# One queue for the first weights of a gated feed-forward block, and a wait ahead of ScalarE's slices of x

## The chip, the cores and the metric

The kernel runs on one core of a Trainium2 chip. A core has a matrix engine (TensorE, PE in the profile, with its weight loads shown apart as PEld), a vector engine (VectorE, DVE), a scalar engine (ScalarE, ACT), a general engine (GpSimd, POOL) and an engine for synchronisation (SyncE, SP). Each engine works through its own program in order. SyncE, ScalarE and GpSimd also issue DMAs, each on a queue of its own; in the profile q1 is SyncE's queue, q10 ScalarE's and q0 GpSimd's. All queues are served by the same 16 DMA engines.

The metric is the device time of one execution, in microseconds (us). Before the change the median of three runs is 300.24 us (299.82 to 303.81).

## The reference

```python
B, S, D, F = 32, 32, 1024, 3584
# x: (B, S, D), w_gate and w_up: (D, F), w_down: (F, D), all bfloat16
def reference(x, w_gate, w_up, w_down):
    return (_gelu(x @ w_gate) * (x @ w_up)) @ w_down
```

With 1024 rows of x, this is two products 1024 x 1024 x 3584, a GELU (tanh form), an elementwise product, and one product 1024 x 3584 x 1024.

## The kernel before, in words

**Tiling.** The contraction over D is cut into 8 k-slices of 128. F is cut into 28 column chunks (m) of 128; chunks 0 to 7 (the "leading eight") have their weights in two large buffers, `wgbig` for gate and `wubig` for up, each loaded in eight DMAs of 256 KB, one per k-slice (`load_w0`, L285). The other twenty chunks come later, in groups of four, 1 MB per load. Rows of x are cut into pieces: XA (rows 0 to 255), XB1 and XB2 (128 rows each), XC2 (rows 512 to 1023).

**Getting x transposed.** TensorE needs x with the contraction index on the partitions. XA is loaded as two blocks of 128 rows (`xa`, one by SyncE, one by ScalarE, L290), turned on TensorE by products with an identity matrix (L351), and copied out of PSUM by VectorE (four copies) and ScalarE (one copy) at L300. The later pieces are loaded in four strips (L281), two strips per "side": SyncE brings side 0, ScalarE side 1, two DMAs per piece, so six for each of the two. VectorE then turns them with transposes at L460, one instruction per k-slice and piece, each waiting for both sides of its piece.

**The order of TensorE's work** is written out by hand in `steps`. After some warm-up products: the turning of XA; then chunks 0 to 7 on XA, all chunks together for k-slice 0, then for 1, and so on to 5, gate before up within a slice; then slices 6 and 7 chunk by chunk (parts 0 to 7). Then parts 8 to 11 (chunks 0 to 3 on rows 256 to 511): k-slices 0 to 3 first for XB1 alone (matmuls of 128 columns), then for XB2, and so on; after that everything part by part with 512 columns. Part 8 and those after it need the PSUM banks of parts 0 to 7 back, which VectorE frees. The second product, with `w_down`, follows (L417).

**ScalarE and VectorE behind it.** For every part ScalarE computes the GELU of the gate product into one of four buffers (L436), and VectorE multiplies it with the up product into `hT` (L469). VectorE's order is a list too (`mix`): E0 E1 E2 E3 (multiplications of parts 0 to 3), then A0 to A3 (XB1's transposes for k-slices 0 to 3), B0 to B3 (XB2's), E4, D4, D5 (both at once), and so on, later mixed with C0 to C7 (XC2's).

**The early loads.** `early_loads` is a generator that SyncE runs with side 0 and ScalarE with side 1. Each of the two loads its block of XA, then eight weight slices (SyncE gate, ScalarE up), then its strips of XB1, XB2 and XC2. A generator step ends at each `yield`; ScalarE counts the steps and after the ninth (`ACT_EARLY`), that is after its weights and ahead of its strips, does its PSUM copy. Nothing makes an x load wait. After its early loads ScalarE goes on to the GELUs, SyncE to the later weight groups, of which the first waits until all of x has landed.

Of the kernel before, what the change touches and what calls it, by code (L numbers as in the profile page):

```python
# [8 lines left out]
ACTF = mybir.ActivationFunctionType  # L9
# [75 lines left out]
def bass_standalone__geglu_ffn__sampling_kernel(  # L85
# [13 lines left out]
    DK = D // P  # L99
# [29 lines left out]
    XPIECES = [XB1, XB2, XC2]  # L129
    XA_PS = [(3, 0, 1), (4, 1, 2), (5, 2, 4), (6, 4, 6), (7, 6, 8)]  # L130
    XA_ACT = (4,)
    ACT_EARLY = 9


    parts = []
# [67 lines left out]
    def evac_eng_is_act(ji):  # L203
        return ji % 2 == 0
# [14 lines left out]
    Q_W0 = {(w, k): _Clock(f"{w}0k{k}", 16) for k in range(DK) for w in ("wg", "wu")}  # L219
# [8 lines left out]
    ctx = _Ctx()  # L228

    with ExitStack() as es:  # L230
# [8 lines left out]
        xa = hT[:, FM - 10:FM - 8, :]  # L239
# [38 lines left out]
        def load_x(ew, eng, q, side):  # L278
            c0, c1 = q[0] // 32, q[1] // 32
            for a in (2 * side, 2 * side + 1):  # L280
                v = ew.do(lambda: eng.dma_start(  # L281
                    xs[32 * a:32 * (a + 1), c0:c1, :], x_r[a, :, c0:c1, :]), clock=Q_X[(q, side)])
            ctx.set(("x", q, side), v)

        def load_w0(ew, eng, w, k):  # L285
            ctx.set((w + "0", k), ew.do(lambda: eng.dma_start(  # L286
                big[w][:, k, :], w_r[w][:, k, 0:NBIG * P]), clock=Q_W0[(w, k)]))

        def early_loads(ew, eng, side):
            yield ctx.set(("xa", side), ew.do(lambda: eng.dma_start(  # L290
                xa[:, side, :], xa_r[:, side, :]), clock=Q_XA[side]))
            for k in range(DK):
                yield load_w0(ew, eng, ("wg", "wu")[side], k)
            for q in XPIECES:
                yield load_x(ew, eng, q, side)

        def xa_copy(ew, j, copy):
            bank, k0, k1 = XA_PS[j]
            ew.wait(C_PE, ctx.get(("XP", j)))
            ctx.set(("XA", j), ew.do(lambda: copy(  # L300
                xT[:, k0:k1, XA[0]:XA[1]],
                ps[:, bank, 0:256 * (k1 - k0)].rearrange("p (k t) -> p k t", t=256))))
# [23 lines left out]
        def prog_sp(eng):  # L326
            sp = _Eng(ctx, eng, None)
            for _ in early_loads(sp, eng, 0):
                pass
            wd_mine = [k for k in range(len(wd_groups)) if k % 2 == 0]  # L330
            for j in range(NG):
                known_chunk = gate_w(sp, j)
                load_w(sp, eng, "wg", j)
                issue_wd(sp, eng, wd_mine, known_chunk, Q_WD_SP)
            issue_wd(sp, eng, wd_mine, FM, Q_WD_SP, force=True)
            ctx.set("wd_sp_total", Q_WD_SP.n)
            last = None
            for ji, (tc, col0, ncols, b) in enumerate(jobs):
                sp.wait(C_ACT if evac_eng_is_act(ji) else C_DVE, ctx.get(("E", ji)))
                last = sp.do(lambda: eng.dma_start(  # L340
                    out_r[:, tc, col0:col0 + ncols],
                    osb[:, tc, col0:col0 + ncols]), clock=Q_OUT)
            sp.wait(Q_OUT, last)
# [81 lines left out]
        def prog_act(eng):  # L425
            act = _Eng(ctx, eng, C_ACT)
            act.do(lambda: eng.activation(warm[:, 0:1], const0, ACTF.Gelu_apprx_tanh))
            for n, _ in enumerate(early_loads(act, eng, 1)):
                if n == ACT_EARLY - 1:
                    for j in XA_ACT:  # L430
                        xa_copy(act, j, lambda o, i: eng.activation(o, i, ACTF.Copy))
            for i, (m, t0, t1, (gb, g0, g1), us) in enumerate(parts):
                act.wait(C_PE, ctx.get(("U" if us[0] == gb else "G", i)))
                if i >= NTB:
                    act.wait(C_DVE, ctx.get(("D", i - NTB)))
                ctx.set(("A", i), act.do(lambda: eng.activation(  # L436
                    t_bufs[i % NTB][:, 0:t1 - t0], ps[:, gb, g0:g1], ACTF.Gelu_apprx_tanh)))
            for ji, (tc, col0, ncols, b) in enumerate(jobs):
                if not evac_eng_is_act(ji):
                    continue  # L440
                act.wait(C_PE, ctx.get(("O", ji)))
                ctx.set(("E", ji), act.do(lambda: eng.activation(  # L442
                    osb[:, tc, col0:col0 + ncols], ps[:, b, 0:ncols], ACTF.Copy)))

        def prog_dve(eng):
# [32 lines left out]
        progs = [  # L478
            (prog_sp, nc.sync, "sync"),
            (prog_act, nc.scalar, "scalar"),  # L480
            (prog_pool, nc.gpsimd, "gpsimd"),
            (prog_pe, nc.tensor, "tensor"),
# [44 lines left out]
```

## Time and profile before

| what | value |
|---|---|
| median of three runs | 300.24 us (299.82 to 303.81) |
| profiled execution, whole | 300.12 us |
| its span, first to last instruction | 298.8 us |
| TensorE busy | 295.9 us, 99% of the span |
| VectorE, ScalarE, GpSimd busy | 58.2, 42.0, 7.9 us |
| granted TensorE clock | 1.00 |
| read from HBM, written | 24.12 MB, 2.10 MB |
| weight slice, SyncE's queue, issue to landing | 8.0 us (median of 8) |
| weight slice, ScalarE's queue, issue to landing | 8.4 us (median of 8) |

Busy time is the time in which an engine has an instruction at work; register, semaphore and DMA-issuing instructions don't count. A row of the timeline gives the start in us, the length in us, the engine, the line of the kernel, the operation with the tile it writes and those it reads, and how many instructions of the kind are merged into the row. SPq and ACTq are rows of DMA issues in the programs of SyncE and ScalarE: their length is the time of issuing, not of the transfer. The time from issue to landing is told separately. A bracket gives the idle time just ahead of the row and what ended it. In the DMA views a queue's line gives packets, megabytes, and the share of 16 engines' time that its packets took (packets overlap a little, so it can pass 100%).

### The profile page before, as it was taken

How to read it: one execution, taken by the hardware profiler on the slowest of the kernel's cores; microseconds unless marked ns; L12 is line 12 of the kernel's file. 1: busy time of each engine (PE TensorE's matmuls, PEld its weight loads, DVE VectorE, ACT ScalarE, POOL GpSimd, SP SyncE). 2: the span in 40 equal slices, each digit the busy share in tenths (PEclk: the TensorE clock that was granted, in tenths of full speed). 3: DMA queues.
4: the chain of work that ended last, by engine and by line, in shares of the span. 5: the costliest groups of instructions: out<-in, count | busy, mean ns of one | idle time of the engine just before them, and what ended most of it. 6: DMA issues, size and time to landing. Idle time of an engine off the chain costs nothing.

```text
span 298.8 us, 3511 instructions
## 1 busy us (share of the span) xinstructions
PE 295.9 (99%) x1558; PEld 150.1 (50%) x1558; DVE 58.2 (19%) x96; ACT 42.0 (14%) x76; POOL 7.9 (3%) x14
## 2 busy tenths in 40 slices
PE   8999999999999999999999999999999999999997
PEld 6899744444444444444444444444444444444456
DVE  2069812111112111112211112210000000000000
ACT  2042211112111112111112111110000000000000
POOL 1001001020001002001000000000000000000000
PEclk9999999999999999999999999999999999999999
DMA  7988003957008400942104000000000100010001
GB/s 264 388 192 279 7 1 105 317 171 252 0 0 276 147 0 13 369 181 84 58 0 140 0 2 0 0 0 20 18 18 20 35 18 18 20 35 18 18 20 35
DMA packets 17806, 26.43 MB, mean 88 GB/s; under 512 B 1024, under 2 KB 11392, under 8 KB 17792
## 3 DMA queue, kind: packets, MB, share of 16 engines
q1 hardware_dynamic: 12688, 14.68, 15.3%
q0 software_dynamic: 2176, 8.39, 7.9%
q10 hardware_dynamic: 2928, 3.15, 3.3%
q8 instruction: 12, 0.20, 0.3%
q14 instruction: 2, 0.02, 0.0%
HBM read 24.12 MB, written 2.10 MB: 88 GB/s over the span
## 4 chain that ended last, share of the span: by engine, by line
PE 97%; DMA 2%; SPq 0%; ACT 0%; issue 0%
PE ps L380 64%; PE ps L417 32%; DMA wgbig<-in_w_gate_dram 2%; SPq L286 0%; SPq L290 0%; ACT xT L442 0%
## 5 line engine op out<-in xcount | busy, mean ns | idle before, releaser
L417 PE MATMUL ps<-wd,hT 128*128 128x512 bf16 (+1 forms) x476 | 96.9, 366 | 0.0
L380 PE MATMUL ps<-xT,wgbig 128*128 128x512 bf16 (+2 forms) x400 | 80.1, 337 | 0.1
L380 PE MATMUL ps<-xT,wubig 128*128 128x512 bf16 (+2 forms) x400 | 79.9, 336 | 0.0
L417 PEld LDWEIGHTS ps<-wd,hT 128*128 128x128 bf16 x476 | 46.6, 98 | 50.4
L469 DVE TENSOR_TENSOR hT<-tb,ps 128x512 bf16<-128x512 f32 (+1 forms) x64 | 39.1, 614 | 143.2 <-PE ps L380 143.2
L436 ACT ACTIVATE tb<-ps 128x512 f32<-128x512 f32 (+1 forms) x64 | 34.8, 544 | 157.7 <-PE ps L380 155.8
L380 PEld LDWEIGHTS ps<-xT,wgbig 128*128 128x128 bf16 x400 | 38.2, 98 | 31.8 <-DMA wgbig<-in_w_gate_dram 0.4
L380 PEld LDWEIGHTS ps<-xT,wubig 128*128 128x128 bf16 x400 | 38.1, 98 | 31.5
L380 PE MATMUL ps<-xT,wgsmall 128*128 128x512 bf16 x128 | 30.2, 379 | 0.0
L380 PE MATMUL ps<-xT,wusmall 128*128 128x512 bf16 x128 | 30.2, 379 | 0.0
L475 DVE CAST xT<-ps 128x512 bf16<-128x512 f32 (+1 forms) x8 | 5.3, 658 | 88.1 <-PE ps L417 88.1
L380 PEld LDWEIGHTS ps<-xT,wgsmall 128*128 128x128 bf16 x128 | 12.5, 98 | 15.1
L380 PEld LDWEIGHTS ps<-xT,wusmall 128*128 128x128 bf16 x128 | 12.5, 98 | 15.1
L442 ACT ACTIVATE xT<-ps 128x512 bf16<-128x512 f32 (+1 forms) x9 | 5.2, 573 | 93.1 <-PE ps L417 93.1
L460 DVE STREAM_TRANSPOSE xT<-hT 128x128 bf16<-128x128 bf16 (+2 forms) x20 | 13.2, 702 | 0.0
L275 POOL DMA_DIRECT2D wubig<-in_w_up_dram x3 | 2.7, 884 | 64.4 <-PE ps L380 64.4
L394 PE MATMUL ps<-const-bfloat16-1.0 128*128 128x512 bf16 (+1 forms) x10 | 3.1, 498 | 0.8 <-PEq L512 0.8
L275 POOL DMA_DIRECT2D wusmall<-in_w_up_dram x2 | 2.0, 992 | 46.8 <-PE ps L380 26.0
L300 DVE CAST xT<-ps 128x256 bf16<-128x256 f32 (+1 forms) x4 | 2.0, 550 | 4.6 <-PE ps L351 4.6
L269 POOL DMA_DIRECT2D wd<-in_w_down_dram x3 | 2.3, 766 | 19.1 <-PE ps L380 19.1
L394 PEld LDWEIGHTS ps<-const-bfloat16-1.0 128*128 128x128 bf16 x10 | 1.2, 139 | 2.4 <-issue 2.4
L351 PE MATMUL ps<-ident,hT 128*128 128x128 bf16 x16 | 1.9, 313 | 0.0
(10 smaller groups left out, 4.9 us busy)
## 6 DMA issues: line engine op xcount, KB each, us to landing
wd<-in_w_down_dram SPq DMA_DIRECT2D x4, 1024.0 KB, 11.4
wgbig<-in_w_gate_dram SPq DMA_DIRECT2D x3, 1024.0 KB, 5.8
wubig<-in_w_up_dram POOLq DMA_DIRECT2D x3, 1024.0 KB, 9.7
wd<-in_w_down_dram POOLq DMA_DIRECT2D x3, 1024.0 KB, 11.2
wgbig<-in_w_gate_dram SPq DMA_DIRECT2D x8, 256.0 KB, 8.0
wubig<-in_w_up_dram ACTq DMA_DIRECT2D x8, 256.0 KB, 8.4
wgsmall<-in_w_gate_dram SPq DMA_DIRECT2D x2, 1024.0 KB, 6.8
wusmall<-in_w_up_dram POOLq DMA_DIRECT2D x2, 1024.0 KB, 9.9
```

Of the source, the lines that this page charges most:

```text
L269: ew.do(lambda: eng.dma_start(wd[:, a:b, :], wd_r[:, a:b, :]), clock=clock)
L275: ctx.set((w, j), ew.do(lambda: eng.dma_start(wbuf(w, buf)[:, :, 0:gsz * P], w_r[w][:, :, c0 * P:(c0 + gsz) * P]), clock=q))
L300: ctx.set(("XA", j), ew.do(lambda: copy(xT[:, k0:k1, XA[0]:XA[1]], ps[:, bank, 0:256 * (k1 - k0)].rearrange("p (k t) -> p k t", t=256))))
L351: v = pe.do(lambda: eng.matmul(ps[:, bank, o:o + P], xa[:, b, :].rearrange("p (j k) -> p j k", k=DK)[:, :, dk], ident[:, :], start=(dk == ...
L380: v = pe.do(lambda: eng.matmul(ps[:, bank, f0:f1], wbuf(w, buf)[:, dk, slot * P:(slot + 1) * P], xT[:, dk, t0:t1], start=first, stop=last ...
L394: pe.do(lambda: eng.matmul(ps[:, 0, 0:n], ones_w, ones_x[:, 0:n], start=True, stop=True), mark=False)
L417: v = pe.do(lambda: eng.matmul(ps[:, b, 0:ncols], hT[:, m, tc * P:(tc + 1) * P], wd[:, m, col0:col0 + ncols], start=(m == 0), stop=(m == F ...
L436: ctx.set(("A", i), act.do(lambda: eng.activation(t_bufs[i % NTB][:, 0:t1 - t0], ps[:, gb, g0:g1], ACTF.Gelu_apprx_tanh)))
L442: ctx.set(("E", ji), act.do(lambda: eng.activation(osb[:, tc, col0:col0 + ncols], ps[:, b, 0:ncols], ACTF.Copy)))
L460: v = dve.do(lambda: eng.transpose(xT[:, dk, q[0]:q[1]].rearrange("p (c i) -> p c i", i=32), src))
L469: ctx.set(("D", i), dve.do(lambda: eng.tensor_tensor(hT[:, m, t0:t1], t_bufs[i % NTB][:, 0:t1 - t0], ps[:, ub, u0:u1], ALU.mult)))
L475: ctx.set(("E", ji), dve.do(lambda: eng.tensor_copy(osb[:, tc, col0:col0 + ncols], ps[:, b, 0:ncols])))
```

## The change

SyncE's early loads become: its block of XA, then sixteen weight slices, gate and up in turn for k-slices 0 to 7, then its strips of x. ScalarE's become: its block of XA, its PSUM copy, a wait until the up weights of k-slice 6 have landed, then its strips of x; it loads no weights of the leading chunks. The bytes loaded, their destinations, TensorE's order and VectorE's order stay as they were. "The chunk-6 weights" of the change's short description are k-slice 6 of the up weights, the semaphore of `("wu", 6)`.

```diff
-    ACT_EARLY = 9
...
         def early_loads(ew, eng, side):
-            yield ctx.set(("xa", side), ew.do(lambda: eng.dma_start(
+            ctx.set(("xa", side), ew.do(lambda: eng.dma_start(
                 xa[:, side, :], xa_r[:, side, :]), clock=Q_XA[side]))
-            for k in range(DK):
-                yield load_w0(ew, eng, ("wg", "wu")[side], k)
+            yield
+            if side == 0:
+                for k in range(DK):
+                    for w in ("wg", "wu"):
+                        load_w0(ew, eng, w, k)
+            else:
+                ew.wait(Q_W0[("wu", 6)], ctx.get(("wu0", 6)))
             for q in XPIECES:
-                yield load_x(ew, eng, q, side)
+                load_x(ew, eng, q, side)
...
         def prog_act(eng):
             act = _Eng(ctx, eng, C_ACT)
             act.do(lambda: eng.activation(warm[:, 0:1], const0, ACTF.Gelu_apprx_tanh))
-            for n, _ in enumerate(early_loads(act, eng, 1)):
-                if n == ACT_EARLY - 1:
-                    for j in XA_ACT:
-                        xa_copy(act, j, lambda o, i: eng.activation(o, i, ACTF.Copy))
+            for _ in early_loads(act, eng, 1):
+                for j in XA_ACT:
+                    xa_copy(act, j, lambda o, i: eng.activation(o, i, ACTF.Copy))
```

## The prediction

> **What bounds the kernel now.** First the page's busy times and its chain, to see which engine sets the end.
>
> ```profile
> PE 295.9 (99%) x1558; PEld 150.1 (50%) x1558; DVE 58.2 (19%) x96; ACT 42.0 (14%) x76; POOL 7.9 (3%) x14
> ...
> PE 97%; DMA 2%; SPq 0%; ACT 0%; issue 0%
> ```
>
> TensorE is busy 295.9 of 298.8 us, and the chain that ended last is 97% TensorE. Only the 2% called DMA can be won, and the change touches nothing after about 30 us. So next comes that chain in order of time, for the first 40 us:
>
> ```profile
> 1.64 6.10 DMA wgbig<-in_w_gate_dram
> 7.74 0.05 issue
> 7.79 32.28 PE ps L380 x299
> ```
>
> The gate weights of k-slice 1 were issued at 1.64 and landed at 7.74; from there TensorE runs without a break. The timeline prices this wait and shows the place where TensorE next comes close to one:
>
> ```profile
> 7.04 0.60 PE L380 MATMUL ps<-xT,wubig 128*128 128x256 bf16 x4
> 7.78 0.77 PEld L380 LDWEIGHTS ps<-xT,wgbig 128*128 128x128 bf16 x8 [0.42 <-DMA wgbig<-in_w_gate_dram]
> ...
> 17.16 3.44 ACT L436 ACTIVATE tb<-ps 128x256 f32<-128x256 f32 x8 [10.78 <-PE ps L380]
> ...
> 17.58 1.73 DVE L469 TENSOR_TENSOR hT<-tb,ps 128x256 bf16<-128x256 f32 x4 [11.02 <-PE ps L380]
> ...
> 19.23 2.41 DVE L460 STREAM_TRANSPOSE xT<-hT 128x128 bf16<-128x128 bf16 x8
> ...
> 19.91 0.32 PEld L380 LDWEIGHTS ps<-xT,wgbig 128*128 128x128 bf16 x4
> 20.02 0.39 PE L380 MATMUL ps<-xT,wgbig 128*128 128x128 bf16 x4
> ```
>
> In brackets stands the idle time before an instruction and its releaser: TensorE lost 0.42 us at 7.78. The other rows are a relay. ScalarE starts the first GELU at 17.16, when part 0 leaves TensorE; VectorE multiplies parts 0 to 3 (E0 to E3) and only then turns the second piece of x (the 128x128 transposes from 19.23). The first of these ends at 19.63 (0.40 us), and TensorE's weight load at 19.91 needs it: 0.28 us of slack. Whatever delays the first GELU by more than about that much delays TensorE.
>
> Last, who issues what:
>
> ```profile
> 2.18 3.33 ACTq L286 DMA_DIRECT2D wubig<-in_w_up_dram  x6
> ...
> 5.12 6.88 SPq L281 DMA_DIRECT2D hT<-in_x_dram  x6
> ...
> 5.79 6.59 ACTq L281 DMA_DIRECT2D hT<-in_x_dram  x6
> ```
>
> ScalarE's issues end at 12.38, in its idle time; the GELU at 17.16 doesn't feel them. That cover is what the change uses up.
>
> **The change, part by part.** The profiled execution took 300.12 us: span 298.80 and 1.32 around it. The median of the runs is 300.24, so I sum against 300.12 and expect a median about 0.1 above it.
>
> 1. *Eight up-weight loads leave ScalarE's queue and stand between SyncE's eight gate loads.* SyncE's cadence was 0.47 us per weight issue (1.17, 1.64, 2.10); k-slice 7 of the up weights is issued at 1.17 + 15 x 0.47 = 8.2 instead of 4.78. Transfers take longer than issues: 256 KB at 384 GB/s (the mean of both queues from 5 to 14 us) are 0.68 us. So the queue stays full and issuing is hidden. TensorE eats one such load in 8 matmuls of 0.109 us = 0.87 us, so it falls behind only if a load takes over 0.87.
>
> Can one queue carry what two did? No row has one queue alone with load behind load. The nearest are moments within one load: ScalarE's queue (q10) with 2 KB packets from 4.4 to 4.8 us, and SyncE's (q1) with 1 KB packets from 24.5 to 26.5 us.
>
> ```profile
> DMA packets 84, 0.15 MB, mean 379 GB/s; under 512 B 10, under 2 KB 10, under 8 KB 84
> q10 hardware_dynamic: 74, 0.14, 98.2%
> ```
>
> ```profile
> DMA packets 721, 0.74 MB, mean 369 GB/s; under 512 B 0, under 2 KB 721, under 8 KB 721
> q1 hardware_dynamic: 721, 0.74, 105.6%
> ```
>
> One queue alone fills the 16 engines (98% and 106%) at 379 and 369 GB/s. Bounds: no cost (384), or half rate as when two shared (1.36 us per load, the third rival). I take none, as both rows are near 384.
>
> 2. *Order of arrival.* Gate and up slice 1 shared the engines and landed at 7.74 and 7.93. In one queue the gate slice comes first and the up slice at the same 7.93, so gate slice 1 lands up to 0.68 us before that, about 7.25. TensorE is free for it at 7.78 - 0.42 = 7.36. **Gain: up to 0.42 us**; nothing if this load's tail is that of one slow engine. What is late next is up slice 1: needed at 7.36 + 0.87 = 8.23, there at 7.93. After that the margin grows by 0.19 us per load.
>
> 3. *ScalarE's new wait for up slice 6.* Behind it on ScalarE stand six x issues and then all GELUs; VectorE's E0 waits for those, and TensorE for VectorE. The copy from PSUM at 5.79 stays ahead of it and keeps its time. When does up slice 6 land? It was issued at 4.25 and took 10.5 us: 14.7. The same bytes go before it now, so 14.7 again; lower bound 14.2 (the gate slice beside it), upper bound 16.8, the landing of the very last weights (4.78 + 12.0), which shared with x and with a 16 KB instruction packet that held one engine for 1.13 us from 14.46.
>
> 4. *Six issues at the wrong moment.* Their row before:
>
> ```profile
> L281 ACTq DMA_DIRECT2D hT<-in_x_dram x6: 391/490/4026, 5.8 to 8.4; - x6
> ```
>
> Five took 0.39 to 0.57 us at a cadence of 0.51; the sixth sat 4.0 us. I leave that out. Per DMA engine a weight, XA or XB load makes 8 packets and a closing one, an XC2 load 33; for ScalarE's queue that is 183 x 16 = 2928, the page's count. At SyncE's fifth x issue 150 were out and 27 landed, so 123 waiting did not block it; ScalarE's queue now holds at most 4 x 9 + 2 x 33 = 102. So six take 5 x 0.51 + 0.48 = 3.05 us, from 14.75 to 17.80; at the shortest duration, 0.39 each, 2.4.
>
> 5. *Sum.* First GELU at 17.83 instead of 17.16. No row shows GELUs with work waiting: a cadence between 0.38 (whole duration, no overlap) and 0.30 (VectorE's two multiplications at 24.31, where work waited); I take 0.34, midway. The fourth GELU starts at 17.83 + 3 x 0.34 = 18.85 (before: 18.475), the first transpose 0.755 later as before, at 19.60, and ends at 20.00. TensorE's load goes at 20.05 instead of 19.91: **+0.14 us**. The 0.42 won earlier is then spent: TensorE comes at 19.50 and waits 0.55. So the time follows ScalarE's chain alone, and is 300.12 + 0.14 = 300.26, in the runs 300.2 to 300.4. Bounds: all gain kept, 299.7; slice 6 at 16.8, 302.2.
>
> Behind this point nothing adds up: transposes come every 0.30 us, and TensorE takes 0.45 per k-slice.
>
> 6. *x itself.* ScalarE's second piece (128 KB) is issued by 15.7. From below: the first loads of x took 3.0 to 3.3 us from issue to landing with empty queues, so 18.4. From above: the rows of x took 10.3 to 13.8 us, but behind all weights of their queue; now nothing is ahead in their own, and from 15 to 20 us the two queues got equal shares (1411 and 1390 packets, 272 GB/s together). At 136 GB/s, 128 KB take 1 us. Needed at 19.60: hidden by about 1 us. If it were not, the last of all x (21.9, when SyncE's next load was released) would set TensorE back 2.4 us, to 302.6; equal sharing excludes that. The last x is wanted at 24.93 and has 3 us to spare.
>
> [...]
>
> **The rivals.**
>
> - *ScalarE isn't late (gain kept).* With slice 6 at 14.2 and issues of 0.39 us the GELUs start at 16.7, and the 0.42 stays: 299.7 us. For it: x no longer mixes into the last weights. Against: it needs both lower bounds. 0.16.
> - *ScalarE later by a microsecond or more.* Slice 6 falls to the tail that the last weights showed (last engine over 1 us behind the others), landing at 15.3 to 16.8; each us goes straight to TensorE at 19.9: 300.8 to 302.2. 0.18.
> - *One queue can't carry it (slower).* A pause at the end of every load, which the other queue used to fill. It decides from 0.19 us per load on, when a load takes over 0.87 and TensorE waits at every slice; slice 6 and the GELUs move by 14 pauses. At half rate, 14 x 0.68 = 9.5 us: 309.7; a pause of 0.43 costs the 6 us that make 2%. Against it the two rows above. 0.04.
> - *The change doesn't do what it says:* gate slice 1 still lands at 7.74. The stall at 7.78 stays, and by the sum the time is the same 300.26, as ScalarE's chain decides; it lies within the forecast.
>
> **How the numbers follow.** Forecast (299.9 to 300.7): 0.62; the rivals 0.16, 0.18 and 0.04. Predicted is the forecast's 300.2. Range 299.5 to 302.2: both bounds, and 0.2 below for the scatter between runs. About 2% (6 us) is what a measurement of this kernel tells from no change; only the third rival reaches that. Faster 0.01, same 0.95, slower 0.04.
>
> **What would show it.** Right: no bracket at 7.78 (gate slice 1 at or before 7.4); an idle bracket of some 0.5 us with a VectorE releaser at the first 128x128 weight load near 20.0; no issue on ScalarE's queue from 1.2 to 14.7 us, then six until 17.8; first GELU near 17.8. Wrong: brackets with DMA releasers at several k-slices (one queue too slow), or the first GELU before 17.2 (gain kept) or after 18.5 (second rival).

## The result, and the profile after

The changed kernel takes 302.37 us (median of 22 runs, 301.88 to 304.14) against 300.43 us for the kernel before (22 runs). The ratio is 1.0063, 95% interval 1.0046 to 1.0079: 1.9 us slower. That is inside the 2% called "same", clear of the scatter, and 0.17 us above the top of the predicted range.

The profiled execution took 303.14 us, with a span of 301.8, so it lies 0.8 us above its median; its span is 3.0 us longer than that of before. In the chain of the changed kernel in order of time (start us, us, what) the early part is no longer TensorE alone:

```profile
7.71 6.53 DMA wubig<-in_w_up_dram
14.23 0.02 issue
14.26 0.33 ACTq L280
14.59 0.03 issue
14.62 7.78 DMA hT<-in_x_dram
...
22.50 0.41 DVE xT L463
...
23.05 14.21 PE ps L384 x160
```

Read it from below: TensorE goes on at 23.05 after a transpose at 22.50, and that one could not begin before ScalarE's second strip of x had landed, 7.78 us after its issue at 14.62. ScalarE had been let go at 14.23 by up slice 6. The timeline of the same execution has the brackets:

```profile
7.13 0.86 PEld L384 LDWEIGHTS ps<-xT,wgbig 128*128 128x128 bf16 x8
...
14.26 3.08 ACTq L280 DMA_DIRECT2D hT<-in_x_dram  x6
...
16.63 0.10 PEld L384 LDWEIGHTS ps<-xT,wgbig 128*128 128x128 bf16 x1 [0.67 <-DMA wgbig<-in_w_gate_dram]
...
18.21 0.10 PEld L384 LDWEIGHTS ps<-xT,wubig 128*128 128x128 bf16 x1 [1.47 <-DMA wubig<-in_w_up_dram]
...
18.54 3.44 ACT L439 ACTIVATE tb<-ps 128x256 f32<-128x256 f32 x8 [12.60 <-PE ps L384]
...
22.50 2.41 DVE L463 STREAM_TRANSPOSE xT<-hT 128x128 bf16<-128x128 bf16 x8 [1.81 <-DMA hT<-in_x_dram]
23.01 0.24 PEld L384 LDWEIGHTS ps<-xT,wgbig 128*128 128x128 bf16 x4 [1.74 <-DVE xT L463]
```

Slice 1 of the gate weights is met without a wait, 0.65 us earlier than before (7.13, not 7.78). Then three waits appear where there was none: 0.67 and 1.47 us for the gate and up weights of k-slice 7, and 1.74 us for the first transposes of XB1. Together 3.88, less 0.65, is 3.2 us; the first 128-column product indeed moved by 3.0 us, from 20.02 to 23.05. The chain has none of the two waits for slice 7: had slice 7 come in time, TensorE would have reached XB1 earlier and waited there until 23.0 all the same. The GELUs begin at 18.54 because part 0 is late, not because ScalarE was busy issuing: its issues ended at 17.34.

Where was x meanwhile? The DMA view of the kernel before from 15 to 20 us, then that of the changed kernel from 15 to 17.8 us (in a queue's line: packets, MB, share of 16 engines' time):

```profile
DMA packets 2801, 1.36 MB, mean 272 GB/s; under 512 B 159, under 2 KB 2796, under 8 KB 2801
...
q10 hardware_dynamic: 1411, 0.69, 59.9%
q1 hardware_dynamic: 1390, 0.67, 59.6%
```

```profile
DMA packets 1018, 0.51 MB, mean 182 GB/s; under 512 B 54, under 2 KB 1007, under 8 KB 1018
...
q1 hardware_dynamic: 1018, 0.51, 122.8%
```

Before, both queues moved x side by side. Now only SyncE's queue (q1) moves it, at 182 GB/s instead of 272; ScalarE's queue (q10), which has had work since 14.26, doesn't appear. Its first packet of x starts at 17.90.

### The profile page after: what moved, and what is told of

It is laid out like the page before. It is cut to its first block, busy times and chain, and to the rows that moved or that the text cites. A ratio compares the mean times of both kernels' runs of the same rounds, so it can differ in the third digit from the quotient of the medians.

```text
span 301.8 us, 3487 instructions
## 1 busy us (share of the span) xinstructions
PE 294.6 (98%) x1534; PEld 149.3 (49%) x1558; DVE 58.3 (19%) x96; ACT 42.0 (14%) x76; POOL 7.9 (3%) x14
## 3 DMA queue, kind: packets, MB, share of 16 engines
q10 hardware_dynamic: 1776, 1.05, 1.8%
## 4 chain that ended last, share of the span: by engine, by line
PE 91%; DMA 5%; SPq 2%; issue 1%; DVE 0%; ACT 0%; ACTq 0%; DVEq 0%
PE ps L384 59%; PE ps L421 32%; DMA hT<-in_x_dram 3%; DMA wubig<-in_w_up_dram 2%; SPq L285 2%; DVE xT L463 0%; SPq L289 0%; ACT xT L445 0%; ACTq L280 0%; DVEq L41 0%
## 5 line engine op out<-in xcount | busy, mean ns | idle before, releaser
L384 PEld LDWEIGHTS ps<-xT,wusmall 128*128 128x128 bf16 x128 | 12.5, 98 | 15.1
L384 PEld LDWEIGHTS ps<-xT,wgsmall 128*128 128x128 bf16 x128 | 12.5, 98 | 15.1
L268 POOL DMA_DIRECT2D wd<-in_w_down_dram x3 | 2.3, 763 | 19.1 <-PE ps L384 19.1
L355 PEld LDWEIGHTS ps<-ident,hT 128*128 128x128 bf16 x16 | 1.3, 153 | 0.2 <-issue 0.2
## 6 DMA issues: line engine op xcount, KB each, us to landing
wd<-in_w_down_dram SPq DMA_DIRECT2D x4, 1024.0 KB, 11.3
```

What stands on the lines that cost most here:

```text
L268: ew.do(lambda: eng.dma_start(wd[:, a:b, :], wd_r[:, a:b, :]), clock=clock)
L384: v = pe.do(lambda: eng.matmul(ps[:, bank, f0:f1], wbuf(w, buf)[:, dk, slot * P:(slot + 1) * P], xT[:, dk, t0:t1], start=first, stop=last ...
```

## The experiments

Theory A after this reading: the loss lies in x, not in the weights. ScalarE's strips stand behind all of SyncE's, and each side by itself moves slowly because it fills one half of the partitions. Its main rival: one queue for all weights is the cost. Times below are medians, ratios are against the kernel before on the same chip.

**e1: the other pairing of strips.** The kernel before, with the two queues at work at once but in the same half of the partitions.

```diff
-            for a in (2 * side, 2 * side + 1):
+            for a in (side, side + 2):
```

> The kernel before with one edit: SyncE brings strips 0 and 2 of each later x piece and ScalarE strips 1 and 3, instead of 0 and 1 against 2 and 3. Queues, sizes, counts and issue times stay. Before, both queues worked at once, one on partitions 0 to 63 and one on 64 to 127, and x moved at 272 GB/s from 15 to 20 us. In the changed kernel SyncE's queue moved x alone, into partitions 0 to 63 only, at 156 to 205 GB/s. Theory A (the half of the partitions limits the rate): here both queues fill the same half at the same time, the rate of x falls to about 200 GB/s, all of x has landed at 23.5 to 24.5 us instead of 21.9, time 300 to 301.5 us. Theory B (one queue alone is slow with 512-byte packets): two queues are at work as before, 270 to 290 GB/s, all of x in at about 21.9, time 300.4 us.

Measured: 300.58 us, ratio 1.0004 (0.9988 to 1.0020). The DMA view from 15 to 20 us:

```profile
DMA packets 2032, 1.03 MB, mean 206 GB/s; under 512 B 143, under 2 KB 2000, under 8 KB 2031
...
q1 hardware_dynamic: 1017, 0.51, 60.6%
q10 hardware_dynamic: 1014, 0.51, 60.0%
```

Two queues share evenly, and still x moves at 206 GB/s instead of 272; all of it had landed at 25.0 us, not 21.8 (theory A had said 23.5 to 24.5). So the half of the partitions sets this rate, not the number of queues. The time hardly feels it, as XB1 was complete at 19.1, still ahead of its use. By what means a half sets it, no view shows.

**e2: the wait alone.** The kernel before, weights on two queues, ScalarE's x behind the wait.

```diff
+            if side == 1:
+                ew.wait(Q_W0[("wu", 6)], ctx.get(("wu0", 6)))
             for q in XPIECES:
```

> The kernel before with the wait alone: weights on two queues as before, ScalarE waits for its up slice 6 ahead of its x strips. Theory A (x is the loss: ScalarE's strips wait behind SyncE's backlog of x, whichever queue the weights took): XB1 complete at 20 to 23 us, TensorE idle 1 to 3 us ahead of the first 128-column products, time 301.5 to 303.5. Theory B (the loss comes from putting all weights on one queue): 300.4 us, with no new idle time.

Measured: 302.70 us, ratio 1.0061 (1.0043 to 1.0079): the whole loss, without the single queue. Its timeline has the same late strip (L462 are the transposes):

```profile
21.90 1.27 DVE L462 STREAM_TRANSPOSE xT<-hT 128x128 bf16<-128x128 bf16 x4 [1.58 <-DMA hT<-in_x_dram]
22.41 0.24 PEld L382 LDWEIGHTS ps<-xT,wgbig 128*128 128x128 bf16 x4 [1.51 <-DVE xT L462]
```

ScalarE issued at 15.04, and its first x packet moved at 18.60.

**e3: the single queue without the wait.**

```diff
-            else:
-                ew.wait(Q_W0[("wu", 6)], ctx.get(("wu0", 6)))
```

> The changed kernel without the wait: all leading weights on SyncE's queue, ScalarE issues its x strips from about 6 us, right after its PSUM copy. Theory A (one queue is enough for the weights, the wait makes the loss): XB1 is in before 19 us and no VectorE wait remains; ScalarE's 768 KB of x now run beside the weights and push the last of them back by up to 768 KB / 390 GB/s = 2 us, so TensorE waits for weights somewhere in slices 3 to 7, 0 to 1.5 us in all: 299.8 to 301.5. Theory B (one queue as such): 302.4, as the changed kernel.

Measured: 303.96 us, ratio 1.0088 (1.0054 to 1.0122). Theory A's 301.5 is passed; the median of four runs lies above theory B's 302.4, too, but the interval holds the changed kernel's 1.0063, so the time alone does not refute B. The trace gives another cause than the single queue: ScalarE's x, issued from 5.65, ran beside the weights from 9.23 on; from slice 4 on a weight load landed every 1.0 us instead of 0.67, and TensorE waited 3.16 and 1.40 us for slice 7 (the profiled execution was a long one, 306.37 us, at a granted clock of 0.989). So the order of x against the weights matters more than I had thought, in both directions.

**e4: both engines wait.** The changed kernel; SyncE holds its x for up slice 6, too.

```diff
                     for w in ("wg", "wu"):
                         load_w0(ew, eng, w, k)
+                ew.wait(Q_W0[("wu", 6)], ctx.get(("wu0", 6)))
             else:
```

> The changed kernel with one more wait: SyncE too waits for up slice 6 before its x strips, so that the x of both sides starts at the same time and nothing of x stands ahead of ScalarE's strips. Theory A (SyncE's x backlog, working on one half of the partitions, holds up ScalarE's strips and the last weights): gate and up slice 7 land at 15 to 16.3 instead of 16.6 and 18.2, x moves at 270 GB/s again, XB1 is in by 18.5, no VectorE wait: 299.7 to 300.6. Theory B (the late issue by itself makes x late, 7.8 us from issue to landing): XB1 at 22, 301.5 to 302.5.

Measured: 300.37 us, ratio 0.9989 (0.9979 to 1.0000). Adding a second wait takes the loss away. From the timeline:

```profile
6.57 0.33 PEld L385 LDWEIGHTS ps<-xT,wubig 128*128 128x128 bf16 x4 [0.94 <-DMA wubig<-in_w_up_dram]
...
14.59 3.62 ACTq L280 DMA_DIRECT2D hT<-in_x_dram  x6
...
18.26 2.44 ACT L440 ACTIVATE tb<-ps 128x256 f32<-128x256 f32 x8 [12.16 <-PE ps L385]
...
20.53 0.24 PEld L385 LDWEIGHTS ps<-xT,wgbig 128*128 128x128 bf16 x4 [0.53 <-DVE xT L464]
```

ScalarE issues 0.3 us later than in the changed kernel, yet its first x packet moves at 15.78, 1.2 us after the issue, and XB1 is complete at 18.0. What remains behind is the relay of the prediction's step 5, where theory A had expected no wait: issues until 18.2, first GELU at 18.26, and 0.53 us lost by TensorE. The row at 6.57 is a wait that the prediction did not have, 0.94 us for up slice 0, so TensorE comes to the relay at 20.00. Here the GELUs had work waiting: their cadence is (2.44 - 0.38)/7 = 0.29 us.

**e5 and e6: both wait, for up slice 5 or 4.** e4 with another number, in both waits.

```diff
-ew.wait(Q_W0[("wu", 6)], ctx.get(("wu0", 6)))
+ew.wait(Q_W0[("wu", 5)], ctx.get(("wu0", 5)))
```

> As e4, but both engines wait for up slice 5, not 6. In e4 the DMA engines ran nearly dry from 15 to 17 us (0 to 66 GB/s in most slices) and ScalarE's six issues ended at 18.2, so TensorE still lost 0.53 us to the relay at 20.5. Theory A (relay: GELUs start when ScalarE has issued): issues begin near 13.3 and end near 16.8, the relay wait goes; the x packets start near 14.9 and can only touch the last loads: 299.7 to 300.3, at or below e4. Theory B (any x beside the last weights costs as much as in the changed kernel): slice 7 lands at 16.5 to 18, 301 to 302.

> As e4, but both engines wait for up slice 4. Theory A: x packets from about 13.5 us, beside the last four or five loads; 512-byte packets at 270 to 290 GB/s push slice 7 back by 1 to 2 us, TensorE waits for it 0.5 to 1.5 us: 300.2 to 301.5, slower than e5. Theory B (earlier is better throughout): at or below e5.

Measured: 300.38 us, 0.9987 (0.9972 to 1.0003) and 300.45 us, 0.9984 (0.9965 to 1.0002). In e5 the relay wait is gone, as theory A has it: first GELU at 17.15 and no wait at XB1. In e6 the up weights of slice 7 cost 0.19 us, less than the 0.5 to 1.5 expected. Up slice 0 is late in these two as well, by 0.32 and 1.28 us. The three can't be told apart by time.

**e7: both wait, weights on two queues.** The kernel before with the wait for up slice 6 on both sides, e4 without the single queue.

> The kernel before (weights on two queues) with both engines' x strips waiting for up slice 6: e4 without its first part. Theory A (one queue is worth the 0.4 us at gate slice 1, the late issues cost the relay 0.5): the stall of 0.4 near 7.8 is back, TensorE waits for weights and relay as in e4: 300.6 to 301.1. Theory B (the queue is worth nothing): 300.4, as e4.

Measured: 300.61 us, 0.9986 (0.9966 to 1.0006). The stall at slice 1 is back (0.70 us at 8.11) and the relay wait is 0.29. Against e4's 0.9989 the single queue shows neither gain nor loss. TensorE leaves the relay at 20.5 in both, so whatever it wins or loses ahead of it is gone there.

**e8: everything on SyncE.** The changed kernel; SyncE brings all strips of x in the order 0, 2, 1, 3, ScalarE only its block of XA.

```diff
-            else:
-                ew.wait(Q_W0[("wu", 6)], ctx.get(("wu0", 6)))
-            for q in XPIECES:
-                load_x(ew, eng, q, side)
+                for q in XPIECES:
+                    load_x(ew, eng, q)
...
-            for a in (2 * side, 2 * side + 1):
+            for a in (0, 2, 1, 3):
```

> SyncE issues everything after its block of XA: weights as in the changed kernel, then all four strips of each x piece, in the order 0, 2, 1, 3; ScalarE issues only its block of XA and does not wait. Theory A (the changed kernel's loss lies in ScalarE's strips held up behind SyncE's, and the relay): XB1 in by 17 to 18, the first GELU when part 0 is done, no VectorE wait; x at about 200 GB/s, all in by 23 to 23.8; what stays is the last engine of slice 7, 0.3 to 1.5 us: 299.8 to 301. Theory B (one queue for weights and x is too slow): XB1 after 19.5, 301.5 or more.

Measured: 300.33 us, ratio 0.9978 (0.9962 to 0.9994). One queue brings all weights and all of x, at 236 GB/s from 15 to 20 us, XB1 is complete at 18.1, and nothing holds the GELUs. It is the only version whose interval lies below 1, by about 0.7 us in the middle and 0.2 at its edge. What it still loses is 0.78 us at up slice 7.

**e9 and e10: what holds ScalarE's strips?** e9 is the changed kernel with SyncE's two XC2 strips held for up slice 6; e10 is the changed kernel with ScalarE's wait moved to up slice 5.

```diff
             for q in XPIECES:
+                if q == XC2:
+                    ew.wait(Q_W0[("wu", 6)], ctx.get(("wu0", 6)))
                 load_x(ew, eng, q, side)
```

> The changed kernel, but SyncE holds its two XC2 strips (512 of its 768 KB of x) until up slice 6 has landed, too; its XB1 and XB2 strips stay right behind the weights. In the changed kernel the first x packet of ScalarE's queue moved at 17.90 us, 3.6 us after its issue at 14.26; in e4, with nothing of SyncE's x ahead, at 15.78, 1.2 us after its issue at 14.59. Theory A (the delay is SyncE's backlog of x draining first): a third of the backlog, so ScalarE's first x packet by about 16.6, XB1 in by 18.8, 300.2 to 301.0. Theory B (a fixed delay of 3.6 us whenever the other queue has any x ahead): first packet at 17.9, XB1 after 20.5, 301.5 to 302.4.

> The changed kernel with ScalarE's wait moved to up slice 5, about 0.7 us earlier; SyncE as in the changed kernel. Theory A (SyncE's whole backlog drains first): the first x packet of ScalarE's queue stays near 17.5 to 18 although it is issued near 13.5, XB1 in at 21.5 to 22.4, time 301.9 to 302.5. Theory B (a fixed delay after the issue): first packet at 17.1, XB1 in 0.7 earlier than in the changed kernel, 301.3 to 301.8.

Measured: e9 301.14 us, 1.0004 (0.9968 to 1.0041), so unclear by time; e10 302.02 us, 1.0059 (1.0042 to 1.0075). The first packets in the traces tell more. With a third of the backlog ahead, ScalarE's first x packet moves at 15.59, 1.5 us after its issue at 14.12, and from 15.5 to 18 us both queues are at work:

```profile
DMA packets 1167, 0.58 MB, mean 230 GB/s; under 512 B 65, under 2 KB 1160, under 8 KB 1167
...
q1 hardware_dynamic: 894, 0.45, 91.8%
q10 hardware_dynamic: 273, 0.12, 27.3%
```

With the issue moved forward to 13.16 and the whole backlog ahead, it moves at 18.55 (theory A had said 17.5 to 18), 5.4 us after it. The DMA view of e10 from 15 to 18.5 us has one queue only:

```profile
DMA packets 1199, 0.61 MB, mean 175 GB/s; under 512 B 69, under 2 KB 1178, under 8 KB 1199
...
q1 hardware_dynamic: 1199, 0.61, 123.1%
```

A delay fixed to the issue is ruled out; it is the backlog that was issued earlier.

Theory A's own numbers for XB1 in e9 were missed: it was complete at 19.98, not by 18.8, although all but the last of the 16 DMA engines had brought their parts by 18.64, and VectorE waited for XB1 and again for XB2:

```profile
20.07 1.27 DVE L465 STREAM_TRANSPOSE xT<-hT 128x128 bf16<-128x128 bf16 x4 [0.26 <-DMA hT<-in_x_dram]
...
22.10 1.28 DVE L465 STREAM_TRANSPOSE xT<-hT 128x128 bf16<-128x128 bf16 x4 [0.75 <-DMA hT<-in_x_dram]
```

In e10 XB1 was complete at 22.17, within the forecast, but TensorE came late itself and did not wait for it; what it lost in that execution (303.99 us, a granted clock of 0.994) stands at slice 7:

```profile
17.55 0.10 PEld L384 LDWEIGHTS ps<-xT,wgbig 128*128 128x128 bf16 x1 [1.30 <-DMA wgbig<-in_w_gate_dram]
...
19.02 0.10 PEld L384 LDWEIGHTS ps<-xT,wubig 128*128 128x128 bf16 x1 [1.36 <-DMA wubig<-in_w_up_dram]
```

**e11: ScalarE's wait at up slice 3.** The changed kernel with that number alone.

> The changed kernel with ScalarE's wait moved to up slice 3 (landing near 8.9 us), so that its x strips are issued right when SyncE has issued its last weights (8.69 in the changed kernel) and in turn with SyncE's strips (from 9.18). In the runs so far ScalarE's first x packet moved when all but 11 to 20 packets per DMA engine of what SyncE had issued earlier were done. Theory A (the two queues are served in the order of issue): ScalarE's first x packet waits for the weights issued before it, 14.0 to 15.0 us, about 5.5 us after its issue; the weights keep their times to slice 6; both halves of x move together as before (250 to 290 GB/s), XB1 in by 17.5 to 18.3, GELUs not held up: 299.7 to 300.5. Theory B (the queues take turns once both have work): first x packet at 10 to 10.5, slices 5 to 7 late as in the run without a wait, 302 to 304.

Measured: 300.65 us, ratio 0.9998 (0.9984 to 1.0012): the loss is gone. I had named the wrong landing: up slice 3 lands at 10.09, so ScalarE issued from 10.11, in turn with SyncE. Its first x packet moved at 13.76. Taking turns would have given about 11.3 (10.11 and the 1.2 us of e4); theory A's 14.0 was 0.2 too late. The weights kept their 0.67 us (up slice 7 alone cost 0.49 us of waiting), XB1 was complete at 18.4, and both halves moved together again from 15 to 20 us:

```profile
DMA packets 2870, 1.40 MB, mean 280 GB/s; under 512 B 162, under 2 KB 2863, under 8 KB 2870
...
q1 hardware_dynamic: 1470, 0.72, 61.3%
q10 hardware_dynamic: 1400, 0.68, 58.0%
```

## Why the prediction was wrong

- **Step 1, one queue carries the weights: right.** From 5 to 14 us q1 moved 386 GB/s, with 104% of the engines' time, and the loads landed 0.65 to 0.70 us apart (0.68 forecast). The rival of a pause at the end of every load is refuted.
- **Step 2, the stall at 7.78 goes: right in the profile.** Gate slice 1 landed at 6.82, earlier than the 7.25 forecast. Of the 0.65 us, 0.42 is the stall; TensorE also began its gate products 0.23 us earlier (5.21), which is not the change's doing: in the other runs with all weights on one queue they began anywhere from 5.12 (e9) to 5.66 (e11). Left out was up slice 0, now second in the same queue: TensorE waited for it 0.94 us in e4, 0.32 in e5, 1.28 in e6 and 0.40 in e9, not in the changed kernel's profile (and 0.23 us in e1, on two queues). That nothing ahead of the relay remains behind it, as step 5 had it, is what e4 against e7 shows.
- **Steps 3 and 4: right.** Up slice 6 landed at 14.23 (14.7, bound 14.2); six issues took 3.08 us (3.05), none was blocked.
- **Step 5, the relay: right, but not what decided.** The changed kernel hides it behind later waits; e4 shows it bare: 0.53 us (0.55), with a GELU cadence of 0.29 (0.34). That the wait agrees so well is in part luck: in e4 TensorE came at 20.00, not 19.50, after its wait for up slice 0, and was released at 20.53, not 20.05, as the issues ended at 18.2 and not 17.8. The upper bound of the sum is also wrong by itself: slice 6 at 16.8 makes 300.26 + 2.1 = 302.4, not 302.2. The measured 302.37 lies at that bound for another reason.
- **Step 6, x itself: the step that failed.** It said that equal sharing of the queues excludes a late XB1, and struck the other end, 302.6 us, from the sum. XB1 was complete at 22.4 instead of the forecast 18.4, and TensorE lost 1.74 us; e2 shows the same (21.8 and 1.51 us), e10 the same late XB1 (22.2). The equal shares from 15 to 20 us, which I took for a property of the queues, came from the times of issue: SyncE and ScalarE had issued x in turn from 5.1 to 8.4. In the changed kernel SyncE's x was issued by 12.5 and ScalarE's after 14.2, and they were served one after the other. A row was carried to a state that it did not show.
- **A term that the sum lacked: slice 7, 0.67 + 1.47 us in this execution.** Step 2 said that the margin grows with every load. It holds for 15 of 16 engines: gate slice 7 had landed on 15 engines by 14.95 and on the last at 16.59, up slice 7 by 15.96 and at 18.17. The 16 KB instruction packet of step 3 (here 1.05 us from 13.93, in the kernel before 1.13 us from 14.46) falls into this. A wait for the gate weights of slice 7 shows where x in flight went to one half alone (the changed kernel 0.67, e10 1.30, e2 0.88, e9 0.35, e1 0.38, e3 3.16) and in none of those where both halves moved together (before, e4, e5, e6, e7, e8, e11). That the busy half delays the late engine fits all of these; no view tells which engine it is or which partitions it fills, so this stays argued. The lag reaches x, too: in the changed kernel's profile the last of XB1 had landed on 15 engines by 20.70 and on the last at 22.40, so up to 1.7 us of its lateness in that execution are the lag, the rest is the order. In e2 the lag there was 0.27 us (21.53 and 21.80), and the loss by time was the same, so the order is enough for it. How the 1.9 us of the medians divide is not shown, as one execution of each kernel was profiled.
- **The rival "ScalarE later by a microsecond or more" came near the size, 300.8 to 302.2, for another reason:** slice 6 was on time.

## What to carry to other kernels

Holding a load back until "the engines are free" put it behind nearly everything that the other queue had issued by then: the first packet of the held strips moved 3.6 us after its issue in the changed kernel, and 1.2 us after it in e4, where nothing of x stood ahead. When two queues must deliver in step, let them issue in step: a second wait (e4), an earlier one (e11) or a single queue (e8) each took the 1.9 us away. And check which partitions a stream fills: two streams to opposite halves moved 272 GB/s together (the kernel before) and 182 where one went alone ahead of the other (the changed kernel).

## What the hardware showed that I had not expected

- **Two queues were served nearly in the order of issue.** When ScalarE's first x packet moved, all but 20 packets for each DMA engine of what SyncE had issued earlier were done in the changed kernel, 20 in e2, 19 in e10, 11 in e3, out of 90 to 255. In e11 it moved sooner, with some 39 of 180 left, while the last two weight loads were under way, so the order is not strict. Packets that are in motion together did share (e1: 1017 and 1014 from 15 to 20 us), but in the changed kernel no packet of ScalarE's queue moved from 14.26 to 17.90 us. What in the path keeps the order, the runs don't tell, as no view shows when ScalarE's packets had reached the DMA engines.
- **One half of the partitions: 175 to 206 GB/s (e10, the changed kernel 182, e1); both together: 272 to 280 GB/s on two queues (the kernel before, e11)** and 236 on one (e8), from 15 to 20 us or a part of it, with the same 512-byte packets.
- **A weight stream on one queue is as fast as on two:** 386 against 384 GB/s from 5 to 14 us.
